# Urgent routings with keys in PSUM and counts against constants, single warming products, a token table written as rows

## The chip, the core and the metric

The kernel runs on one core of a Trainium2 chip. The metric is the device time of one execution in microseconds (us). Engines: PE (TensorE, with its weight loads as PEld), DVE (VectorE), ACT (ScalarE), POOL (GpSimd), SP (SyncE, which starts most DMAs). Each works through its own instructions in the order in which they are written; semaphores hold an instruction back until what it needs is there.

## The reference

Attention over 4 x 8 heads of 576 positions of width 64, mixed with a linear memory by a gate per head, gives 2304 tokens of width 512. A first expert layer routes each token to one of 8 experts, by the largest scores first and with at most 288 tokens an expert; then a gated MLP works on all tokens.

```python
a /= a.sum(-1, keepdims=True) + 1e-09
local = np.matmul(a, v)
g = 1.0 / (1.0 + np.exp(-beta))[None, :, None, None]
return (g * mem_out + (1 - g) * local)
...
order = np.argsort(-flat)                 # all token-expert scores, best first
for idx in order:
    tok, e = (int(idx) // E, int(idx) % E)
    if assigned[tok] >= 0 or counts[e] >= cap:
        continue
    assigned[tok] = e
    counts[e] += 1
...
out[mask] = np.maximum(x[mask] @ w1[e], 0.0) @ w2[e]
...
g = x @ w_gate
return (g / (1.0 + np.exp(-g)) * (x @ w_val)) @ w_out
```

## The kernel before

**Stages.** Attention over 16 pairs of heads runs from 0 to about 249 us. Then the greedy assignment is done in eight phases. Phase `ph` finds, over the scores that are still alive, the expert that fills up next, and its 288 tokens (`route`, L983 on). The tokens of a phase are gathered by an indirect DMA (`xg`), transposed on PE (L1451) to `xt`, and go through that expert's two products. Groups of finished tokens then go through the gated MLP and are scattered to the output. Products of fp32 numbers are made as three products of fp32r parts: `ws` (L1262 on ACT, L1266 on DVE or POOL) holds a weight's upper part and its difference.

**A routing.** The scores become integer keys `kx`, whose upper 16 bits make `h` (L1033), 128 partitions of 160 values. A search in base 4 then finds the key of rank 288, digit by digit: 16 rounds, 8 on the upper half and 8 on the lower. A round counts the keys over three thresholds. One count is a Sign with an accumulator on ACT (L1047), two are comparisons with an accumulator on DVE (L1053). Two products on PE with the stationaries `grp` and `ngrp` add up the counts of an expert's partitions (L1058, L1059). DVE compares the totals with 288 (`kj`, L1063), which adds to the sum found so far (column 3 of `gain`), and makes the next thresholds `th` from it (L1069). After round 7, L1074 turns the keys to the lower half. At the end DVE writes the token numbers, `ix` (L1204), 96 x 3, and SP writes them to the table `tbl` in HBM (L1421), from which the scatters' lists `gi` are read later (L1316).

**Order.** A planner inside the program (`Op`, `Slot`, `schedule`) takes each step with its engine, its duration by a table, what it depends on and which buffer slots it takes, and writes all engines' orders when the program is built. `HARDS` = 2: the first two routings, which nothing can replace, are urgent (`near` in the new code) and their steps go ahead of other work. Buffers in PSUM: `rp` (one tile of 512 columns for all routing steps), `wkp` (three), `acc`. Of the readers and writers of one PSUM tile each waits for the one before it where the program's semaphores order them.

**Warming.** At the start 28 products with `identb` (a unit matrix of bf16, L94) as stationary stand first on PE (L973). In route 1 `warm` (L1271) puts 12 such products as one step, and 2 later, ahead of the first expert's products.

**Start.** DVE makes `ident`, `identb` and other constants, 96 single memsets of `steps` and 16 of `gain` (L111 to L117), the counts' buffers `cn`, and then the gate `gt` from beta (L149 to L156), with one exponential on ACT (L150) between. The first values of `am`, turned by PE in L570, give DVE the scales of the heads (L576 to L579).

Of the kernel before, what the change touches and what calls it, by code (L numbers as in the profile page):

```python
# [9 lines left out]
F32 = mybir.dt.float32  # L10
# [64 lines left out]
def kernel(ctx: ExitStack, tc: tile.TileContext, qt_, kt_, v, M_prev, z_prev, beta,  # L75
# [12 lines left out]
    with tc.tile_pool(name="tmp", bufs=1) as tmp:  # L88
# [4 lines left out]
        identb = cst.tile([128, 128], BF, name="identb")  # L93
        V.tensor_scalar(identb, jp, 0.0, None, op0=OP.is_equal)  # L94
# [12 lines left out]
    steps = [cst.tile([128, 16, 3], F32, name=f"steps{y}") for y in range(2)]  # L107
# [4 lines left out]
    for r in range(16):  # L112
        w = 4.0 ** (7 - r)
        V.memset(gain[:, r, 0:3], w)
        for j in range(3):
            for y in range(2):
                V.memset(steps[y][:, r, j:j + 1], (j + 1) * w - (0.0 if j > y else 0.5 if r < 8 else 2.0 ** -17))  # L117
# [4 lines left out]
    cnts = [[cst.tile([128, 4], BF, name=f"cn{x}{y}") for x in range(2)] for y in range(2)]  # L122
    sgns = [cst.tile([128, 2], BF, name=f"sg{x}") for x in range(2)]
    for y in range(2):
        for x in cnts[y]:
            V.memset(x, float(CAP))
            V.memset(x[:, 0:y + 1], 80.0)
# [331 lines left out]
    with ExitStack() as actx:  # L459
# [5 lines left out]
        G.iota(jw, pattern=[[1, 128]], base=0, channel_multiplier=-1, allow_small_or_imprecise_dtypes=True)  # L465
        maskb = wk.tile([128, 128], BF, name="maskb", bufs=1)
# [521 lines left out]
    def route(ph, prev):  # L988
# [10 lines left out]
        def rp():  # L999
            return Slot("rp", 1)  # L1000
# [26 lines left out]
        def f(e):  # L1027
# [7 lines left out]
        step("A", 0.24, f)  # L1035
# [4 lines left out]
        na = 1  # L1040
        for rd in range(16):
            sp_ = rp()

            def f(e, rd=rd):
                with nc.allow_low_precision(reason="whole numbers up to 160"):
                    for j in range(na):
                        A.activation(t.jk2, t.R, AF.Sign, scale=-1.0, bias=t.th[:, j:j + 1] if rd % 8 else steps[na - 1][:, rd, j:j + 1],  # L1047
                                     accum_out=sgns[rd % 2][:, j:j + 1])
            sgn = Op(None, {"A": 0.49 * na}, f, deps=[last[0]], hard=ph < HARDS, lat=SAFE if ph else 0.0, slack=RND if ph else 0.0)

            def f(e, rd=rd):
                for j in range(na, 3):
                    V.tensor_scalar(t.junk, t.R, t.th[:, j:j + 1] if rd % 8 else (j + 1) * 4.0 ** (7 - rd), None,  # L1053
                                    op0=OP.is_ge, op1=OP.add, accum_out=cnts[na - 1][rd % 2][:, j:j + 1])
            cnt = step("V", (0.37 if rd % 8 else 0.3) * (3 - na), f, lat=SAFE if ph else 0.0, slack=RND if ph else 0.0)

            def f(e, rd=rd):
                PE.matmul(ptile()[:, 0:4], grp, cnts[na - 1][rd % 2], start=True, stop=False)  # L1058
                PE.matmul(t.p[:, 0:na], ngrp, sgns[rd % 2][:, 0:na], start=False, stop=True)  # L1059
            step("PE", 0.08, f, deps=[sgn], take=[sp_])  # L1060
# [5 lines left out]
            if (rd + 1) % 8:  # L1066
                def f(e, rd=rd):
                    t.th = rt.tile([128, 4], F32, name="th", bufs=2)
                    V.tensor_scalar(t.th[:, 0:3], steps[na - 1][:, rd + 1], gain[:, rd + 1, 3:4], None, op0=OP.add, op1=OP.add,  # L1069
                                    accum_out=t.th[:, 3:4])  # L1070
                step("V", 0.22, f)
            elif rd == 7:
                def f(e):
                    V.scalar_tensor_tensor(t.h[2], t.h[1], t.kd[:, 1:2], t.h[0], op0=OP.subtract, op1=OP.add)  # L1074
                    t.R = t.h[2]
                step("V", 0.25, f, deps=[low_], port="V")
# [538 lines left out]
```

## Time and profile before

| | |
|---|---|
| median of three runs | 1049.97 us (1046.54 to 1054.10) |
| the profiled execution | 1046.89 us, of which the span is 1045.1 us |
| busy in the span | PE 925.2 us, DVE 773.2, ACT 591.9, POOL 357.9 |
| TensorE's granted clock | .939 of full speed on average |
| stages | attention to about 249 us, route 0 to 291, route 1 to 346, then experts and groups |

The span is the time from the first to the last instruction that the profile shows. Busy shares are means over stages with different limits: PE's 89% is nearly full after 360 us and low between 250 and 291, so each part of the change is to be held against its own stage.

### The profile page before, as it was taken

How to read it: one execution, taken by the hardware profiler on the slowest of the kernel's cores; microseconds unless marked ns; L12 is line 12 of the kernel's file. 1: busy time of each engine (PE TensorE's matmuls, PEld its weight loads, DVE VectorE, ACT ScalarE, POOL GpSimd, SP SyncE). 2: the span in 40 equal slices, each digit the busy share in tenths (PEclk: the TensorE clock that was granted, in tenths of full speed). 3: DMA queues.
4: the chain of work that ended last, by engine and by line, in shares of the span. 5: the costliest groups of instructions: out<-in, count | busy, mean ns of one | idle time of the engine just before them, and what ended most of it. 6: DMA issues, size and time to landing. Idle time of an engine off the chain costs nothing.

```text
span 1045.1 us, 19428 instructions
## 1 busy us (share of the span) xinstructions
PE 925.2 (89%) x6909; PEld 783.5 (75%) x6909; DVE 773.2 (74%) x2633; ACT 591.9 (57%) x1304; POOL 357.9 (34%) x498
## 2 busy tenths in 40 slices
PE   7689889875168699997999999999999999999995
PEld 4468778774048597775898777899777899888895
DVE  8878888895857788989977676878786766444462
ACT  7758979763445377446566445466544555433552
POOL 4467677750245474455421232230011140000200
PEclk9979999997569699998999999999999999999998
DMA  9569789764462733265350033260032170000100
GB/s 278 109 140 228 166 202 181 167 138 127 140 144 62 184 102 101 61 175 170 120 146 2 1 121 24 95 151 21 1 121 24 44 202 21 1 1 1 41 1 21
DMA packets 130545, 105.37 MB, mean 101 GB/s; under 512 B 99136, under 2 KB 112592, under 8 KB 128400
## 3 DMA queue, kind: packets, MB, share of 16 engines
q1 hardware_dynamic: 120560, 61.14, 24.4%
q0 software_dynamic: 9888, 43.00, 15.4%
q8 instruction: 54, 0.88, 0.4%
q14 instruction: 43, 0.35, 0.1%
HBM read 72.39 MB, written 9.45 MB: 78 GB/s over the span
## 4 chain that ended last, share of the span: by engine, by line
PE 48%; issue 1%; POOL 1%; DMA 1%; DVE 0%; ACT 0%; POOLq 0%
PE wkp L1233 29%; PE acc L1233 18%; DMA xg<-xs,ix 1%; PE wkp L1451 1%; POOL out_dram L1386 1%; PE rp L1197 0%; DVE ws L1266 0%; POOL r L1251 0%; POOL xg L1251 0%; PE rp L1059 0%; PE rp L1058 0%; DVE hd L1484 0%; PE rp L1090 0%; ACT ws L1262 0%; ACT f64r L1381 0%
## 5 line engine op out<-in xcount | busy, mean ns | idle before, releaser
L1233 PE MATMUL wkp<-ya,ws 128*128 128x512 f32 (+1 forms) x864 | 182.4, 364 | 1.3 <-ACT ws L1262 1.3
L1233 PE MATMUL acc<-ws,us 128*128 128x512 f32 x648 | 162.2, 395 | 0.0
L1233 PEld LDWEIGHTS wkp<-ya,ws 128*128 128x128 f32 x864 | 143.4, 192 | 24.3 <-ACT ws L1262 1.4
L1266 DVE TENSOR_TENSOR ws<-m2r,ws 128x512 fp32r<-128x512 f32 x141 | 99.6, 707 | 71.6 <-ACT ws L1262 69.7
L1262 ACT ACTIVATE ws<-m2r 128x512 fp32r<-128x512 f32 x170 | 106.6, 628 | 78.6 <-PE wkp L1233 41.9
L1233 PE MATMUL wkp<-yb,ws 128*128 128x512 f32 x576 | 137.9, 393 | 0.0
L1233 PEld LDWEIGHTS acc<-ws,us 128*128 128x128 f32 x648 | 118.4, 188 | 22.5
L1233 PEld LDWEIGHTS wkp<-yb,ws 128*128 128x128 f32 x576 | 106.4, 188 | 21.1
L1233 PE MATMUL acc<-hd,ws 128*128 128x288 f32 x768 | 120.4, 304 | 0.6 <-DVE hd L1484 0.6
L1233 PE MATMUL wkp<-xt,ws 128*128 128x288 f32 x768 | 120.2, 304 | 0.3 <-DVE xt L1456 0.3
L783 POOL TENSOR_TENSOR pb<-P,pb 128x576 f16<-128x576 f32 (+2 forms) x61 | 93.2, 1529 | 52.4 <-ACT pb L776 43.9
L1233 PEld LDWEIGHTS acc<-hd,ws 128*128 128x128 f32 x768 | 108.9, 193 | 1.8 <-DVE hd L1484 1.2
L1233 PEld LDWEIGHTS wkp<-xt,ws 128*128 128x128 f32 x768 | 109.1, 193 | 1.3 <-DVE xt L1456 0.6
L1262 ACT ACTIVATE ws<-r 128x512 fp32r<-128x512 f32 x128 | 79.6, 645 | 38.2 <-PE acc L1233 12.2
L1266 DVE TENSOR_TENSOR ws<-r,ws 128x512 fp32r<-128x512 f32 x114 | 78.3, 700 | 19.7 <-ACT ws L1262 14.6
L1053 DVE TENSOR_SCALAR_CACHE_REDUCE junk<-h,th 128x160 bf16<-128x160 f32 x224 | 84.8, 379 | 7.0
L1047 ACT ACTIVATE jk<-h,th 128x160 bf16<-128x160 f32 x112 | 47.6, 425 | 59.0 <-DVE th L1069 58.6
L1386 POOL DMA_INDIRECT out_dram<-f64r,gi x18 | 20.0, 1113 | 165.7 <-DVE f64r L1379 119.2
L1343 ACT ACTIVATE sil<-wkp 128x512 f32<-128x512 f32 (+1 forms) x60 | 33.2, 553 | 75.4 <-PE wkp L1233 56.5
L1251 POOL DMA_INDIRECT r<-in_moe_w_dram,wi x32 | 33.5, 1047 | 119.7 <-DVE key L1080 54.8
L452 POOL TENSOR_TENSOR m2r<-f64a,f64r 128x512 int32<-128x512 int32 x34 | 46.6, 1372 | 72.2 <-DVE kj L1063 32.4
L675 PE MATMUL sp<-kt,qt 64*128 64x288 f32 (+4 forms) x576 | 57.0, 324 | 14.4 <-ACT P L720 7.4
(230 smaller groups left out, 1685.3 us busy)
## 6 DMA issues: line engine op xcount, KB each, us to landing
f<-in_moe_w_out_dram SPq DMA_DIRECT2D x12, 512.0 KB, 3.6
f<-in_moe_w_gate_dram SPq DMA_DIRECT2D x11, 512.0 KB, 4.0
f<-in_moe_w_val_dram SPq DMA_DIRECT2D x11, 512.0 KB, 3.5
vr<-in_vb_dram SPq DMA_DIRECT2D x16, 320.0 KB, 4.4
xq<-in_qt_dram SPq DMA_DIRECT2D x16, 288.0 KB, 4.3
xk<-in_kt_dram SPq DMA_DIRECT2D x16, 288.0 KB, 4.0
xs<-X SPq DMA_DIRECT2D x3, 1024.0 KB, 5.1
pt<-pb SPq DMA_TRANSPOSE x49, 4.2
```

Source lines behind the costliest of these rows:

```text
L452: return op({"G": 1.225}, lambda e: G.tensor_tensor(dst.bitcast(I32), t.a, t.r, op=OP.add), [o1] + o4, use=[ra, aa])
L675: PE.matmul(dst, st, mv, start=k not in keys[:j], stop=k not in keys[j + 1:])
L783: lambda e, i=i, c=c: (V if e == "V" else G).tensor_tensor(p.pb[i][:, 1, c], p.P[i][:, c], p.pb[i][:, 0, c], op=OP.subtract), deps=[ho], u ...
L1047: A.activation(t.jk2, t.R, AF.Sign, scale=-1.0, bias=t.th[:, j:j + 1] if rd % 8 else steps[na - 1][:, rd, j:j + 1], accum_out=sgns[rd % 2] ...
L1053: V.tensor_scalar(t.junk, t.R, t.th[:, j:j + 1] if rd % 8 else (j + 1) * 4.0 ** (7 - rd), None, op0=OP.is_ge, op1=OP.add, accum_out=cnts[n ...
L1233: PE.matmul(dst, st(x), mv(y), start=first and t == 0, stop=last and t == 2)
L1251: G.indirect_dma_start(out=dst, out_offset=None, in_=src, in_offset=bass.IndirectOffsetOnAxis(ap=idx, axis=0))
L1262: A.activation(h.t[:, 0], raw(), AF.Copy)
L1266: (V if e == "V" else G).tensor_tensor(h.t[:, 1], raw(), _f(h.t[:, 0]), op=OP.subtract)
L1343: A.activation(t.sl, t.g[0][:, 0:n], AF.Silu)
L1386: put = G.indirect_dma_start(out=out, out_offset=bass.IndirectOffsetOnAxis(ap=self.gi[:, q:q + 1], axis=0), in_=t.o, in_offset=None)
L1451: PE.transpose(t.p[:, TW * j:TW * j + TW], x.xg[:, j, c:DM:4], ident[0:TW, 0:TW])
```

## The change

In the two urgent routings the thresholds `th` are no longer made in 14 of the 16 rounds. DVE counts where the key less the sum so far is at least a constant of `steps`, by a SCALAR_TENSOR_TENSOR whose second tensor is one column read 160 times. ACT's Sign takes the sum as its bias and reads `xs`, a copy of the negated keys with the round's constant added, which ACT makes anew in each round (L1071 of the new program, an added instruction). The keys `t.R` lie in columns 0 to 160, later 256 to 416, of one PSUM tile, and the round's products go to columns 480 or 496 of the same tile. `steps` exists once, not twice, with 48 memsets; of the buffers `cn` two remain. `identb` is built in the attention part, after `jw`. `warm` makes each product a step of its own, with `grp` as stationary. `ix` is made a second time as floats (`ixf`), turned on PE to 3 x 96, copied to integers (`rows`), and written to the table in three rows of 96 numbers.

```diff
-        identb = cst.tile([128, 128], BF, name="identb")
-        V.tensor_scalar(identb, jp, 0.0, None, op0=OP.is_equal)
...
-    steps = [cst.tile([128, 16, 3], F32, name=f"steps{y}") for y in range(2)]
+    steps = cst.tile([128, 16, 3], F32, name="steps")
...
+        identb = wk.tile([128, 128], BF, name="identb", bufs=1)
+        V.tensor_scalar(identb, jw, 0.0, None, op0=OP.is_equal)
...
+            if near:
+                ptile()
+                t.pk, t.hs, t.h[1] = t.p, list(t.h), t.p[:, 0:160]
...
+                    if past:
+                        A.activation(t.jk2, t.xs, AF.Sign, bias=gain[:, rd, 3:4], accum_out=sgns[rd % 2])
+                    else:
+                        A.activation(t.jk2, t.R, AF.Sign, scale=-1.0, bias=t.th[:, 0:1] if rd % 8 else steps[:, rd, 0:1],
+                                     accum_out=sgns[rd % 2])
...
+                    if past:
+                        V.scalar_tensor_tensor(t.junk, t.R, gain[:, rd, 3:4], steps[:, rd, j:j + 1].to_broadcast([128, 160]),
+                                               op0=OP.subtract, op1=OP.is_ge, accum_out=cnts[rd % 2][:, j:j + 1])
...
+            if near and (rd + 1) % 8:
+                def f(e, rd=rd):
+                    t.xs = t.hs[1 + rd % 2]
+                    A.activation(t.xs, t.R, AF.Copy, scale=-1.0, bias=4.0 ** (6 - rd) - (0.5 if rd < 8 else 2.0 ** -17))
+                base = Op(None, {"A": 0.24}, f, deps=[sgn], hard=True, use=[sk])
...
+                t.p = t.pk[:, 480 + 16 * (rd % 2):] if near else ptile()
+                PE.matmul(t.p[:, 0:4], grp, cnts[rd % 2], start=True, stop=False)
+                PE.matmul(t.p[:, 0:1], ngrp, sgns[rd % 2], start=False, stop=True)
...
-            if (rd + 1) % 8:
+            if (rd + 1) % 8 and not near:
...
+                    if near:
+                        t.h[2] = t.pk[:, 256:416]
...
+            V.tensor_scalar(r.ixf, t.p3[0:TW, 0:3], float(N // 2), None, op0=OP.add)
...
-            for _ in range(n):
-                PE.matmul(p, identb, onesb[:, None, :].to_broadcast([128, 4, 128]), start=True, stop=True)
-        pe(0.24 * n, f, deps, take=[w0])
+        for x in range(n):
+            def f(e, x=x):
+                if x == 0:
+                    t.p = work().rearrange("p (a b) -> p a b", a=4)
+                PE.matmul(t.p, grp, onesb[:, None, :].to_broadcast([128, 4, 128]), start=True, stop=True)
+            o = pe(0.24, f, deps, take=[] if x else [w0], use=[w0] if x else [])
+            deps = [o]
...
+                PE.transpose(t.p[0:3, 0:TW], self.r.ixf, ident[0:TW, 0:TW])
...
+                V.tensor_copy(t.r, t.p[0:3, 0:TW])
...
+                tbl[CAP * s:CAP * s + CAP].rearrange("(a b) -> a b", b=TW), t.r), deps=[o], use=[rs])
```

**Where instructions move.** DVE at the program's start, before (line, operation, written tile <- read tiles, shape):

```order
L92 TENSOR_SCALAR ident<-jp 128x128
L94 TENSOR_SCALAR identb<-jp 128x128
L96 TENSOR_SCALAR before<-jp 128x128
L98 MEMSET onesb 128x128
L101 TENSOR_SCALAR jmod<-jmod 128x128
L103 TENSOR_SCALAR grp<-jmod 128x128
```

The new DVE order holds, of these, all but `identb` at the start; here it follows the last steps of the gate:

```order
L150 TENSOR_SCALAR gt<-gt 128x8
L151 TENSOR_SCALAR gt<-gt 128x8
L152 RECIPROCAL gt<-gt 128x8
L159 MEMSET alive 128x18
L161 MEMSET vw 128x16
L463 TENSOR_SCALAR identb<-jw 128x128
L465 TENSOR_SCALAR maskb<-jw 128x128
```

`identb` has moved from the second of DVE's rows behind six rows of the gate `gt`, which wait for ACT's exponential.

DVE in the first rounds of route 0, before (in brackets the engines whose semaphores a row waits for):

```order
L1053 TENSOR_SCALAR junk,cn_204<-h_4760 128x160 [waits Activation_49]
L1053 TENSOR_SCALAR junk,cn_204<-h_4760 128x160 [waits DVE_49]
L1063 SCALAR_TENSOR_TENSOR kj,gain<-rp,gain 128x4 [waits PE_49]
L1069 TENSOR_SCALAR th<-steps_84,gain 128x3 [waits DVE_49]
L1053 TENSOR_SCALAR junk,cn_205<-h_4760,th 128x160 [waits DVE_49] x2
```

ACT there in the new program; `rp` is the PSUM tile of the keys, `sg` the sums of the Signs, `f64a` and `f64r` conversions of other weights:

```order
L1035 ACTIVATE rp<-kx 128x160 [waits DVE_49,Activation_49]
L1052 ACTIVATE jk_4709,sg_155<-rp,steps 128x160 [waits Activation_49]
L1071 ACTIVATE h_4705<-rp 128x160 [waits DVE_49]
L1039 ACTIVATE h_4704<-kx 128x160
L1050 ACTIVATE jk_4709,sg_156<-h_4705,gain 128x160 [waits DVE_49]
L1071 ACTIVATE h_4706<-rp 128x160 [waits DVE_49,PE_49]
L440 ACTIVATE f64a<-f_4690 128x512 [waits DMAHW2_49]
L434 ACTIVATE f64r<-f_4690 128x512
```

On PE there, in the new program, the round's products wait for ACT alone:

```order
L1009 MATMUL rp<-ident,vw 128x128 [waits DVE_49,PE_49]
L1076 LDWEIGHTS grp
L1076 MATMUL rp<-cn_153,grp 128x4 [waits Activation_49]
L1077 LDWEIGHTS ngrp
L1077 MATMUL rp<-sg_155,ngrp 128x1
```

The row `th` is gone from DVE, and ACT has gained a row of L1071 in each round, which waits for DVE's counts and which PE's pair waits for.

PE in route 1, before, at the first round's pair:

```order
L1011 MATMUL rp<-ident,vw 128x128
L1058 LDWEIGHTS grp
L1058 MATMUL rp<-cn_204,grp 128x4
L1059 LDWEIGHTS ngrp
L1059 MATMUL rp<-sg_208,ngrp 128x1
L1278 LDWEIGHTS identb
L1278 MATMUL wkp<-onesb,identb 128x512
```

The twelve products of L1278 follow one another there, and the next pair stands behind the twelfth. In the new program:

```order
L1300 LDWEIGHTS grp
L1300 MATMUL wkp<-onesb,grp 128x512
L1076 LDWEIGHTS grp
L1076 MATMUL rp<-cn_153,grp 128x4
L1077 LDWEIGHTS ngrp
L1077 MATMUL rp<-sg_155,ngrp 128x1
L1300 LDWEIGHTS grp
L1300 MATMUL wkp<-onesb,grp 128x512
```

Four products now stand ahead of the first pair, four between it and the second, and four behind that; three of the nine transposes of gathered tokens then stand ahead of the third pair, where nine did.

## Rows read from the trace of the kernel before

**Rows 1.** Windows of the span: us, busy us of each engine (instructions), PE's granted clock, DMA.

```profile
250.00:291.00 41.00, 6.05 (x54) 4.30 (x54) 35.37 (x197) 18.84 (x52) 8.12 (x11) 0.52 0.41 128
360.00:440.00 80.00, 79.67 (x443) 67.85 (x442) 69.66 (x236) 55.16 (x122) 43.73 (x59) 0.97 0.35 109
440.00:490.00 50.00, 41.51 (x201) 31.62 (x201) 42.23 (x173) 28.50 (x71) 24.48 (x32) 0.90 0.59 170
```

**Rows 2.** Timeline of the start: us, duration, engine, line, operation, [idle before it <-releaser].

```profile
1.82 8.08 PE L973 MATMUL T<-onesb,identb 128*128 128x512 bf16 x28 [1.82 <-DVE onesb L98]
9.94 0.29 PE L570 MATMUL T<-ident,am 128*128 128x128 f32 x1
5.62 3.79 PEld L973 LDWEIGHTS <-identb 128*128 128x128 bf16 x18 [0.28 <-issue]
6.33 0.21 ACT L150 ACTIVATE gt<-gt 128x8 f32<-128x8 f32 x1 [0.89 <-DVE gt L149]
7.42 0.20 DVE L156 RECIPROCAL gt<-gt 128x8 f32<-128x8 f32 x1
11.78 0.28 DVE L576 TENSOR_REDUCE am<-T 128x1 f32<-128x128 f32 x1
```

**Rows 3.** Waits from 10 to 249 us: total us, times, longest; the row on a DMA.

```profile
PEld L844 <- DMA pt<-pb: 3.9, 3, 2.6
```

**Rows 4.** Timeline of one round of route 0, and `kj` of its last round.

```profile
253.67 0.16 DVE L1063 SCALAR_TENSOR_TENSOR kj<-rp,gain 128x4 f32<-128x4 f32 x1 [0.32 <-PE rp L1059]
254.13 0.38 DVE L1053 TENSOR_SCALAR_CACHE_REDUCE junk<-h,th 128x160 bf16<-128x160 f32 x1
254.19 0.43 ACT L1047 ACTIVATE jk<-h,th 128x160 bf16<-128x160 f32 x1 [0.79 <-DVE th L1069]
254.56 0.38 DVE L1053 TENSOR_SCALAR_CACHE_REDUCE junk<-h,th 128x160 bf16<-128x160 f32 x1
255.01 0.19 PE L1058 MATMUL rp<-cn,grp 128*128 128x4 bf16 x1 [1.39 <-DVE junk L1053]
255.27 0.16 DVE L1063 SCALAR_TENSOR_TENSOR kj<-rp,gain 128x4 f32<-128x4 f32 x1 [0.32 <-PE rp L1059]
255.48 0.21 DVE L1069 TENSOR_SCALAR_CACHE_REDUCE th<-steps,gain 128x3 f32<-128x3 f32 x1
255.73 0.38 DVE L1053 TENSOR_SCALAR_CACHE_REDUCE junk<-h,th 128x160 bf16<-128x160 f32 x1
280.11 0.15 DVE L1063 SCALAR_TENSOR_TENSOR kj<-rp,gain 128x4 f32<-128x4 f32 x1
```

**Rows 5.** One line's instructions (durations in ns: least, median, most), then groups by line and shape.

```profile
L1074 DVE SCALAR_TENSOR_TENSOR h<-h,kd,h x8: 380/385/1265, 266.0 to 797.1; 128x160 f32<-128x160 f32 x8
...
L1024 DVE TENSOR_TENSOR kx<-vb,kx 128x160 int32<-128x160 int32 x8 | 2.6, 326 | 0.3
...
L1539 DVE TENSOR_TENSOR yb<-acc,yb 128x160 fp32r<-128x160 f32 x4 | 1.2, 318 | 0.0
...
L1536 ACT ACTIVATE yb<-acc 128x160 fp32r<-128x160 f32 x4 | 1.2, 305 | 0.0
```

**Rows 6.** Timeline of route 1: warming block, `kj` behind it, gathered tokens, last round.

```profile
294.06 5.27 PE L1278 MATMUL wkp<-onesb,identb 128*128 128x512 bf16 x12
299.44 0.16 DVE L1063 SCALAR_TENSOR_TENSOR kj<-rp,gain 128x4 f32<-128x4 f32 x1 [3.91 <-PE rp L1059]
304.59 0.41 ACT L1454 ACTIVATE xt<-wkp 128x288 fp32r<-128x288 f32 x1 [9.29 <-PE wkp L1451]
305.31 0.21 PE L1058 MATMUL rp<-cn,grp 128*128 128x4 bf16 x1
336.40 0.16 DVE L1063 SCALAR_TENSOR_TENSOR kj<-rp,gain 128x4 f32<-128x4 f32 x1 [0.50 <-PE rp L1059]
```

**Rows 7.** Transposes of the gathered tokens (ns: least, median, most); `ws` differences on DVE.

```profile
L1451 PE MATMUL wkp<-ident,xg x96: 246/286/437, 301.5 to 857.8; 96*128 96x96 f32 x96
...
L1266 DVE TENSOR_TENSOR ws<-m2r,ws 128x512 fp32r<-128x512 f32 x141 | 99.6, 707 | 71.6 <-ACT ws L1262 69.7
```

More of the change, by code (lines that the diff above doesn't have):

```diff
@@ L1041, in route @@
         for rd in range(16):
-            sp_ = rp()
-            def f(e, rd=rd):
[L1045 to L1059, printed above, removed]
@@ L1060, in route, with f @@
-            step("PE", 0.08, f, deps=[sgn], take=[sp_])
+            sp_ = sk if near else rp()
+            past = near and rd % 8 > 0
+            def f(e, rd=rd, past=past):
+                with nc.allow_low_precision(reason="whole numbers up to 160"):
+                    if past:
[3 more added lines that the diff above has]
+                                     accum_out=sgns[rd % 2])
@@ new lines, in route, with f @@
+            sgn = Op(None, {"A": 0.49}, f, deps=[last[0], base], hard=near, lat=SAFE if ph else 0.0, slack=RND if ph else 0.0,
+                     use=[sk] if near and not past else [])
+            def f(e, rd=rd, past=past):
+                for j in (1, 2):
+                    if past:
+                        V.scalar_tensor_tensor(t.junk, t.R, gain[:, rd, 3:4], steps[:, rd, j:j + 1].to_broadcast([128, 160]),
+                                               op0=OP.subtract, op1=OP.is_ge, accum_out=cnts[rd % 2][:, j:j + 1])
+                    else:
+                        V.tensor_scalar(t.junk, t.R, t.th[:, j:j + 1] if rd % 8 else (j + 1) * 4.0 ** (7 - rd), None,
+                                        op0=OP.is_ge, op1=OP.add, accum_out=cnts[rd % 2][:, j:j + 1])
@@ L1062, in f @@
+            step("PE", 0.08, f, deps=[sgn], take=[] if near else [sp_], use=[sk] if near else [])
             def f(e, rd=rd):
@@ L1073, in f @@
                 def f(e):
+                    if near:
+                        t.h[2] = t.pk[:, 256:416]
                     V.scalar_tensor_tensor(t.h[2], t.h[1], t.kd[:, 1:2], t.h[0], op0=OP.subtract, op1=OP.add)
                     t.R = t.h[2]
-                step("V", 0.25, f, deps=[low_], port="V")
+                step("V", 0.35 if near else 0.25, f, deps=[low_], port="" if near else "V", use=[sk] if near else [])
         def f(e):
@@ L1203, in f @@
             r.ix = rt.tile([TW, 3], I32, name="ix", bufs=8)
+            r.ixf = rt.tile([TW, 3], F32, name="ixf", bufs=2)
             V.tensor_scalar(r.ix, t.p3[0:TW, 0:3], float(N // 2), None, op0=OP.add)
-        r.idx = step("V", 0.07, f, use=[s3], slack=RSL)
+            V.tensor_scalar(r.ixf, t.p3[0:TW, 0:3], float(N // 2), None, op0=OP.add)
+        r.idx = step("V", 0.14, f, use=[s3], slack=RSL)
         return r
@@ L1420, in __init__, with f @@
             self.g1.append(gath(4.3, lambda e: load1(e, 1), [self.r.wix], after=late_, take=[r1[1]]))
-            self.told = Op(None, {"D": 0.5}, lambda e: SP.dma_start(
-                tbl[CAP * s:CAP * s + CAP].rearrange("(a b) -> b a", b=TW), self.r.ix), deps=[self.r.idx])
+            ws, rs, t = Slot("wkp", 3), Slot("rows", 1), type("T", (), {})()
+            def f(e):
+                t.p = work()
+                PE.transpose(t.p[0:3, 0:TW], self.r.ixf, ident[0:TW, 0:TW])
+            o = Op(None, {"PE": 0.12}, f, deps=[self.r.idx], after=late_ and [self.g1[1].g], take=[ws])
+            def f(e):
+                t.r = rt.tile([3, TW], I32, name="rows")
+                V.tensor_copy(t.r, t.p[0:3, 0:TW])
+            o = Op(None, {"V": 0.17}, f, deps=[o], take=[rs], use=[ws])
+            self.told = Op(None, {"D": 0.2}, lambda e: SP.dma_start(
+                tbl[CAP * s:CAP * s + CAP].rearrange("(a b) -> a b", b=TW), t.r), deps=[o], use=[rs])
             self.w2 = []
```

26 lines of the change are left out of this document (12 added, 14 removed).

## Prediction

> **What bounds the kernel now.** I read the table of windows first, stage by stage. Up to about 249 us all engines run through one attention schedule, each in a written order. From 360 us on PE is nearly always busy: 79.67 of 80.00 us in 360 to 440, though only 41.51 of 50.00 in 440 to 490 [rows 1]. Between them PE is mostly idle: 6.05 us of work in 41.00 during the first urgent routing [rows 1]. There the chain of a routing round sets the time, not any engine's load. So three things can move the end: when attention gets going, how long the chains of the two urgent routings take, and what PE itself has to do after 360. A shift of the first two arrives whole at the expert work, since its tokens wait for the routings; off PE, a change after 360 costs only where PE waits for it.
>
> **Start: `identb` comes late.** Before, PE's 28 warming products begin at 1.82 and the transpose of L570 follows at 9.94 [rows 2]. In the new order DVE makes their stationary `identb` only behind the sigmoid chain of `gt`, so all 28 wait for that chain. It can't be early: ACT was ready for the exponential .89 us ahead of 6.33 [rows 2], at 5.44. DVE, with 48 memsets fewer, will be there by then. So the last step of the chain, at 7.42 before [rows 2], moves to 6.53, and `identb`, three rows further on, is there at about 6.9; PE begins at about 7.0, 5.2 us later than at 1.82. If its products take what they took, L570's transpose comes at 15.1. DVE read its result at 11.78 [rows 2], after other work; now it waits until about 15.7. That is **+4.0 us**: behind that row stand, on DVE, the scales of the first heads, on ACT `vh`, which is made with them, and so the whole first pair. Bounds: PE's products run at two speeds, the last 18 at .21 us each (3.79 for 18 weight loads [rows 2], the 2.4 GHz level), the first at about twice that; were all 28 at .21, they would end 2.2 us earlier, so +1.8 at least; +5.2 if DVE's other work slips too. Does the slip survive to 249? Only a schedule that waits for loads would take it up. Between 10 and 249 us the largest wait of PE's side for a DMA is 3.9 us, for `pt<-pb` [rows 3], which is attention's own product and slips with it. So I let it pass whole.
>
> **A round of the urgent routings.** Before, undisturbed, counts begin at 254.13 and at 255.73: 1.60 us. It is .43 to the second count, .45 to the pair of products, .26 to `kj` at 255.27, .21 to `th`, .25 to the next count [rows 4]. The edit drops `th`, **−.25**: the count follows `kj` at the .21 at which `th` did. The new count is a SCALAR_TENSOR_TENSOR over 160 columns; one such stands in the trace with a median of 385 ns [rows 5], where the old one has .38 [rows 4]: at most +.02 for two.
>
> Reading keys from PSUM: a DVE TENSOR_TENSOR with one PSUM source and 160 columns takes 318 ns, one with SBUF alone 326 [rows 5]. I charge nothing. The difference, .008, is small; four times it on all 64 counts would be 2.0 us, which I keep as a bound.
>
> The Trainium skill (Perfetto Trace Analysis, "Optimizing Scalar/DVE Operations") puts the overhead of a DVE access at about 60 ns on SBUF and 125 on PSUM. By it 64 counts would cost 64 × .065 = 4.2 us more, an estimate from that page; the two rows here show no such surcharge, and the measurement decides.
>
> What the diff doesn't say is the wait that the bank brings. The keys lie in the same PSUM tile as the round's products, and the order with its waits shows PE's pair waiting for ACT's new Copy, which waits for DVE's second count. So the Copy stands in the chain. Its price: an ACTIVATE from PSUM with 160 columns takes 305 ns [rows 5], and I add .04 for one hand-over more. A round is now .21 + .44 + .455 + .345 + .26 = 1.71: **+.11 where −.23 was to be had**. 14 such rounds a route: +1.5. In rounds 0 and 8 the Sign reads the PSUM keys too and DVE's counts wait for it: .43 [rows 4], with its hand-over about .55, and the Copy's .345 on top: +.9 each, +1.8. Part of this returns. Route 0's `kj` run from 253.67 to 280.11, 15 rounds in 26.44 [rows 4], 1.76 each and not 1.60, since DVE's conversions stand between them; these 2.4 us can now lie under Copy and products. I take 1.3 back: **route 0 +2.0 us**, bounds 0 (all hidden, rounds 0 and 8 at half their price) and +3.5 (nothing hidden).
>
> **Route 1.** Before, PE has twelve warming products in one block from 294.06, for 5.27 us, and round 1's pair sits behind it: `kj` at 299.44 waited 3.91 us for PE [rows 6]. Round 2's Sign stood behind ACT's `xt` at 304.59, which had waited 9.29 us for PE's transposes of gathered tokens, and its pair came at 305.31 [rows 6]. Now the products come in fours, with pairs between them, and the Sign stands ahead of `xt`. But round 2's pair still follows three transposes of the gathered tokens, so most of the 3.91 is lost to the same gather, and the pair comes at about 304.4, 1 us earlier. From there to the last `kj` at 336.40 [rows 6] a round takes 2.4 us, as PE's product blocks and ACT's queue stand in the way. Following the new order with these durations the later pairs stand behind smaller blocks, and the last comes 2 to 4 us earlier, though ACT has .31 more in each round. I take **−3.0**, bounds −6 (the freed 3.91 and the 1 us kept, and another from the later rounds) and +3 (ACT late by .2 in each of 14 rounds).
>
> **After 360.** There are eight transposes of 3x96 for the table. The nearest row, 96x96, has a median of 286 ns [rows 7], with loads overlapped by others; I take .19, for 7 where PE is full: **+1.3**, bounds 0 and 2. Eight `ixf` and eight copies to `rows` on DVE lie under PE. The table written as rows lies under the expert work, since no engine waits for it before the last scatters: 0. Last, the planner moved work: DVE makes 33 more of the `ws` differences (141 become 166 on one path and 114 become 122 on the other, by the order), POOL fewer. At .71 each [rows 7] that is 23 us more for DVE. DVE has 10.3 us free of 80 in 360 to 440 and 7.8 of 50 in 440 to 490 [rows 1], and about ten of the 33 fall there. PE already loses 8.5 us in the second window, so it could lose a few more or fewer: 0, bounds −4 and +8.
>
> **Sum.** 4.0 + 2.0 − 3.0 + 1.3 = +4.3. The profiled execution has 1046.9, so 1051.2. The median of the three runs, 1050.0, lies 3.1 above that execution; I put the forecast between the two bases, at **1053 us**.
>
> **Rivals.**
> *The edits do what they say* (faster). The Copy ends before PE needs the counts, a round loses .23, 3.2 us a route, and route 1 gains its 6 in all; with the start slip at 1.8 that is 1.8 − 3.2 − 6 + 1.3 = −6.1: 1041, and 1036 with 3 to 4 us of PE's stalls in 440 to 490 gone. Against it: the waits in the order. It holds if a round is under 1.55 us.
> *The start slip is taken up inside attention.* 4.3 − 4.0: 1047 to 1050. For it: every engine idles somewhere in attention. Against: hardly a row there waits for an input.
> *DVE becomes the bound after 360* (slower). The ten added differences in 360 to 490 delay PE's operands by .71 each, 7 us, and as much again where conversions queued behind them feed POOL late: 4.3 + 7 to 14: 1058 to 1067. It decides from 14 us of idle PE in the window that answers to 440 to 490. For it: DVE is 84% busy there. Against: POOL is relieved of the same work.
> *PSUM reads are dear for DVE.* .03 a count, as bounded above: +2.0, 1055.
>
> **How the numbers follow.** Forecast .45, edits as they say .13, slip taken up .20, DVE bound .17, dear PSUM .05. A measurement of this kernel can tell about 1%, 10.5 us, from no change. Faster by over 1% is under 1039.5: the lower part of the first rival and the favourable ends of the forecast's bounds, .10. Slower by over 1% is over 1060.5: most of the DVE rival and the forecast's upper tail, .17. Within: .73. The range 1041 to 1063 leaves out the deep part of the first rival and the top of the DVE rival, about .2; the forecast's own range is 1047 to 1059.
>
> **What would show it.** The first product on PE at about 7.0 and DVE's `am` near 15.7; attention's last row 4 us later; ACT's Copy between counts and products in each urgent round, and rounds of 1.7 us where nothing interferes; the last `kj` of route 0 some 6 us later than before, that of route 1 some 3. Wrong would be rounds under 1.55, an unchanged end of attention, or over 14 us of idle PE in the window that answers to 440 to 490.

## The result

The changed kernel is faster, by 1.0%. Twenty runs of each gave medians of 1038.41 us against 1049.05 us before; the ratio is .9902, with a 95% interval from .9879 to .9924. I had forecast 1053 us, practically no change, with 1041 as the lower end. The profiled execution of the changed kernel has a span of 1037.6 us, that of the kernel before 1045.1.

The profile after, windows: us, busy us of PE, PEld, DVE, ACT and POOL with instructions, PE's granted clock, DMA share, GB/s.

```profile
253.00:295.00 42.00, 5.82 (x54) 4.42 (x54) 32.86 (x167) 22.43 (x66) 7.73 (x11) 0.50 0.38 120
360.00:440.00 80.00, 76.03 (x426) 63.41 (x426) 75.21 (x264) 54.65 (x125) 23.16 (x32) 1.00 0.30 93
440.00:490.00 50.00, 47.60 (x240) 37.22 (x240) 44.02 (x176) 31.10 (x72) 21.59 (x29) 0.97 0.52 170
```

Against [rows 1]: the first urgent routing looks as before (5.82 us of PE's work, against 6.05; this window begins 3 us later). PE has lost 3.6 us of work between 360 and 440 and gained 6.1 between 440 and 490, and DVE is fuller in both. PE's granted clock in these two windows went from .97 to 1.00 and from .90 to .97 of full speed.

The start, in the timeline of the changed kernel:

```profile
7.24 8.05 PE L971 MATMUL T<-onesb,identb 128*128 128x512 bf16 x28 [7.24 <-DVE identb L463]
15.12 0.27 PE L568 MATMUL T<-ident,am 128*128 128x128 f32 x1
...
15.43 0.29 DVE L574 TENSOR_REDUCE am<-T 128x1 f32<-128x128 f32 x1 [2.67 <-PE T L568]
```

The three times came out as forecast, to .3 us: first product at 7.24 (7.0), the transpose at 15.12 (15.1), `am` at 15.43 (15.7) after 2.67 us of waiting. Against 11.78 in [rows 2] that is +3.65.

One round of route 0 in the changed kernel, and the last `kj`:

```profile
259.09 0.16 DVE L1081 SCALAR_TENSOR_TENSOR kj<-rp,gain 128x4 f32<-128x4 f32 x1 [0.75 <-PE rp L1077]
...
259.30 0.38 DVE L1060 SCALAR_TENSOR_TENSOR junk<-rp,gain,steps 128x160 bf16<-128x160 f32 x1
...
259.73 0.38 DVE L1060 SCALAR_TENSOR_TENSOR junk<-rp,gain,steps 128x160 bf16<-128x160 f32 x1
...
260.21 0.30 ACT L1071 ACTIVATE h<-rp 128x160 f32<-128x160 f32 x1
...
260.57 0.16 PE L1076 MATMUL rp<-cn,grp 128*128 128x4 bf16 x1 [1.59 <-ACT h L1071]
...
260.88 0.16 DVE L1081 SCALAR_TENSOR_TENSOR kj<-rp,gain 128x4 f32<-128x4 f32 x1 [0.42 <-PE rp L1077]
...
284.15 0.15 DVE L1081 SCALAR_TENSOR_TENSOR kj<-rp,gain 128x4 f32<-128x4 f32 x1
```

The Copy of L1071 (260.21) stands between the second count (259.73) and the products (260.57). A round takes 1.79 us here, where it took 1.60 undisturbed in [rows 4], and 12 of the 15 steps from `kj` to `kj` take 1.78 or 1.79; the other three are the last round of each half, which has no Copy (1.32 and 1.62), and round 8 (2.47). The route's 15 steps take 26.84 us, 26.44 before. The conversions (L442 here) lie under the wait.

Now the row that I had not looked at: the gathers of tokens, `xg`. Each answer has the gather's issue on POOL and its time from issue to landing. Before:

```profile
L1251 POOL DMA_INDIRECT xg<-xs,ix x24: 908/927/1453, 291.5 to 843.5; - x24
...
DMA to landing us min/median/max: 7.0/9.3/10.8
```

After:

```profile
L1273 POOL DMA_INDIRECT xg<-xs,ix x24: 906/925/1448, 295.6 to 835.5; - x24
...
DMA to landing us min/median/max: 3.0/3.4/8.6
```

The median gather lands 3.4 us after its issue, not 9.3. The same view for the table, before and then after:

```profile
L1421 SPq DMA_DIRECT2D tbl<-ix x8: 305/321/338, 291.3 to 839.4; - x8
...
DMA to landing us min/median/max: 6.0/8.1/10.9
```

```profile
L1456 SPq DMA_DIRECT2D tbl<-rows x8: 232/247/323, 303.6 to 879.9; - x8
...
DMA to landing us min/median/max: 2.1/2.6/3.1
```

The first write of the table, issued at 291.3 before, went out just ahead of the first gather, at 291.5; now it is issued at 303.6, when that gather has landed.

To see where the 7.5 us between the two profiled executions went, I cut each at the same five instructions: the first product of the first routing, `ix` of routes 0 and 1, the first product of the first group (`wkp<-ya`), and the last of that group's 288 products of this kind, all of which stand in each trace. The times of these rows give each stage's length in us:

| kernel | attention | route 0 | route 1 | to the group | its 288 products | rest of the span | span |
|---|---|---|---|---|---|---|---|
| before | 250.9 | 40.2 | 54.8 | 42.8 | 113.0 | 543.4 | 1045.1 |
| changed | 253.4 | 41.7 | 49.0 | 44.7 | 105.4 | 543.4 | 1037.6 |
| forecast, difference | +4.0 | +2.0 | −3.0 | part of +1.3 | 0 | part of +1.3 | +4.3 |
| measured, difference | +2.6 | +1.5 | −5.8 | +1.9 | −7.6 | 0 | −7.5 |

The start and route 0 stand about where they were put. Route 1 and the group's products make the result. The group's start moves within the order, so the two stages behind route 1 are best read together: 155.9 us before, 150.1 after.

### The profile page after: what moved, and what is told of

Same layout as the page of the kernel before. It is cut to its first block, busy times and chain, and to the rows that moved or that the text cites. A ratio compares the mean times of both kernels' runs of the same rounds, so it can differ in the third digit from the quotient of the medians.

```text
span 1037.6 us, 19343 instructions
## 1 busy us (share of the span) xinstructions
PE 923.2 (89%) x6917; PEld 785.0 (76%) x6917; DVE 783.5 (76%) x2575; ACT 598.6 (58%) x1331; POOL 312.2 (30%) x432
## 4 chain that ended last, share of the span: by engine, by line
PE 71%; DVE 17%; ACT 7%; issue 2%; DMA 1%; POOL 1%; ACTq 0%; SPq 0%; DVEq 0%; POOLq 0%
PE wkp L1255 37%; PE acc L1255 21%; PE sp L673 3%; PE O L842 2%; DVE ws L1288 2%; ACT P L723 2%; DVE nm L709 2%; DVE junk L1060 1%; PE T L971 1%; PE wkp L1486 1%; DVE f64a L445 1%; DVE nm L707 1%; PE T L902 1%; PE T L807 1%; ACT P L718 1%
## 5 line engine op out<-in xcount | busy, mean ns | idle before, releaser
L1255 PE MATMUL wkp<-ya,ws 128*128 128x512 f32 (+1 forms) x864 | 179.7, 361 | 2.7 <-DVE xt L1491 2.2
L1288 DVE TENSOR_TENSOR ws<-m2r,ws 128x512 fp32r<-128x512 f32 x166 | 115.6, 696 | 69.8 <-ACT ws L1284 67.5
L1284 ACT ACTIVATE ws<-m2r 128x512 fp32r<-128x512 f32 x170 | 106.6, 628 | 80.3 <-PE wkp L1255 41.6
L1284 ACT ACTIVATE ws<-r 128x512 fp32r<-128x512 f32 x128 | 80.0, 647 | 40.8 <-PE acc L1255 15.1
L1288 DVE TENSOR_TENSOR ws<-r,ws 128x512 fp32r<-128x512 f32 x122 | 87.5, 730 | 15.8 <-ACT ws L1284 14.0
L448 POOL TENSOR_TENSOR m2r<-f64a,f64r 128x512 int32<-128x512 int32 x34 | 45.5, 1339 | 113.6 <-DVE f64a L445 45.7
L1366 ACT ACTIVATE sil<-wkp 128x512 f32<-128x512 f32 (+1 forms) x60 | 33.2, 553 | 74.8 <-PE wkp L1255 54.9
L1409 POOL DMA_INDIRECT out_dram<-f64r,gi x18 | 22.6, 1254 | 172.0 <-DVE f64r L1402 119.4
L1063 DVE TENSOR_SCALAR_CACHE_REDUCE junk<-h,th 128x160 bf16<-128x160 f32 x168 | 63.5, 378 | 4.9
L673 PEld LDWEIGHTS sp<-kt,qt 64*128 64x128 f32 x576 | 47.0, 198 | 24.6 <-ACT P L718 11.3
```

Of the source, the lines that this page charges most:

```text
L448: return op({"G": 1.225}, lambda e: G.tensor_tensor(dst.bitcast(I32), t.a, t.r, op=OP.add), [o1] + o4, use=[ra, aa])
L673: PE.matmul(dst, st, mv, start=k not in keys[:j], stop=k not in keys[j + 1:])
L1255: PE.matmul(dst, st(x), mv(y), start=first and t == 0, stop=last and t == 2)
L1284: A.activation(h.t[:, 0], raw(), AF.Copy)
L1288: (V if e == "V" else G).tensor_tensor(h.t[:, 1], raw(), _f(h.t[:, 0]), op=OP.subtract)
L1366: A.activation(t.sl, t.g[0][:, 0:n], AF.Silu)
```

## The experiments

Each was timed beside the kernel before on the same chip, in five rounds; ratios are to the kernel before. Three theories stood against one another. *Table*: the old write of the table, ahead of the gathers, holds them back, and everything else is nearly free or costs. *Warming*: route 1 gains because its pairs no longer stand behind a block. *Routing*: the dropped step pays.

### Each part alone

**The table alone.** The kernel before with the table's write of the changed one. Room in SBUF was needed for it: `steps` once, and `identb` late, with `grp` as stationary of the first products and of the warming block.

```diff
...
-                tbl[CAP * s:CAP * s + CAP].rearrange("(a b) -> b a", b=TW), self.r.ix), deps=[self.r.idx])
...
+                tbl[CAP * s:CAP * s + CAP].rearrange("(a b) -> a b", b=TW), t.r), deps=[o], use=[rs])
...
```

> The kernel before with the table alone written as rows (to make room, steps once, and identb late with grp as stationary of the first products, which leaves the start as it was). If the write of single words is what holds the gathers back, xg lands 3 to 4 us after its issue instead of 9 to 10, no transpose waits for xg, the second route takes some 3 us less from ix to ix, and the order, in which DVE makes 30 more ws differences as in the changed kernel, loses its stalls around 440 to 490: 1037 to 1042. If the gain is the warming's or the routing's: 1047 to 1051, with the landing of xg changed or not.

Measured: 1037.85 us, ratio .9863 (.9817 to .9909). Gathers land 3.2 us after their issue (median), route 1 takes 50.2 us, the stage up to the group 40.8 and its products 110.8. This part alone gives about what the whole change gives; the two intervals overlap.

**All but the table.** The changed kernel with the old write.

```diff
...
-                tbl[CAP * s:CAP * s + CAP].rearrange("(a b) -> a b", b=TW), t.r), deps=[o], use=[rs])
...
+                tbl[CAP * s:CAP * s + CAP].rearrange("(a b) -> b a", b=TW), self.r.ix), deps=[self.r.idx])
...
```

> The changed kernel with the old table write. If the single words hold the gathers back: xg lands 9 to 10 us after its issue, the second route loses 3 us or more of its gain, stalls come back after 434, and the time is 1048 to 1055. If warming or routing carry the gain: 1037 to 1041.

Measured: 1067.67 us, ratio 1.0153 (1.0107 to 1.02). Gathers land after 10.0 us again, route 1 takes 54.9 us, the group's products 122.7 and the rest of the span 549.6. Without the table's part the change is a loss, and a larger one than expected.

**The routing alone**: the kernel before with the new counts, the Copy and the keys in PSUM, and the constants that go with them.

> The kernel before with the new counts in the two urgent routings alone. By the chain of waits a round of route 0 takes 1.78 us as in the changed kernel, route 0 is 1 to 2 us longer than before, and the time is 1048 to 1053. If the dropped step is what pays: 1040 to 1044.

Measured: 1063.38 us, ratio 1.0112 (1.006 to 1.0164). Route 0 takes 41.7 us, 1.5 more than before, as the chain of waits says. The time lies above both expectations: most of the loss stands behind the routes, 8.5 us in the stage up to the group and 7.4 in the rest, where the planner's order has changed and the gathers land late (median 9.9 us). What makes this order dear with late gathers stays open.

**The warming alone**: the kernel before with single products.

```diff
...
-            for _ in range(n):
-                PE.matmul(p, identb, onesb[:, None, :].to_broadcast([128, 4, 128]), start=True, stop=True)
-        pe(0.24 * n, f, deps, take=[w0])
...
+            o = pe(0.24, f, deps, take=[] if x else [w0], use=[w0] if x else [])
...
```

> The kernel before with single warming products alone. If the second route gained because its pairs no longer stand behind a block, it takes 3 to 6 us less from ix to ix and the time is 1043 to 1047. If the gather sets it, round 2 still waits for xg until about 304 us and the time is 1048 to 1051.

Measured: 1058.28 us, ratio 1.0061 (1.0028 to 1.0093). That is above both expectations. Route 1 takes 55.7 us, no less than before, and PE waits for the gather longer; the profiled execution loses the rest behind it, 5.7 us in the group's products and 7.2 in the rest of the span. The first row is of the kernel before, the second of this one, in the waits of PE from 245 to 360 us.

```profile
PE wkp L1451 <- DMA xg<-xs,ix: 8.1, 5, 2.4
```

```profile
PE wkp L1452 <- DMA xg<-xs,ix: 13.8, 5, 5.5
```

So with a late gather the freed time goes to the gather, as the prediction had it. What it lacked was that the gather itself would come early.

### Packets, place or order

The table's part changes three things at once: the packets of the write, its place (behind the gather, since PE and DVE must turn the numbers first), and the planner's order, in which DVE gets 30 more of the `ws` differences. The next four kernels separate them. The first three have PE, DVE, ACT and POOL in exactly the order of the kernel they start from, and SP too except for the write's own form.

**Before, 12 bytes a packet.** Same order as before; the three numbers of a partition go side by side, so 96 packets replace 288. The table's numbering is permuted by it, and with it the places of the output's rows; the sizes of all other transfers stay.

```diff
-                tbl[CAP * s:CAP * s + CAP].rearrange("(a b) -> b a", b=TW), self.r.ix), deps=[self.r.idx])
+                tbl[CAP * s:CAP * s + CAP].rearrange("(b a) -> b a", b=TW), self.r.ix), deps=[self.r.idx])
```

> The kernel before in the same order on every engine; only the table is written with the three numbers of a partition side by side, 96 packets of 12 bytes for 288 of 4 (so the table's numbering, and with it the place of the output's rows, is permuted). If packets ahead of the gather hold it back: xg lands 5 to 7 us after its issue, the second route takes 2 to 4 us less from ix to ix, and the time is 1040 to 1046. If the order made the gain: xg lands as before or the time stays at 1048 to 1053.

Measured: 1035.83 us, ratio .9848 (.9798 to .9898), faster than either expectation. The order of the engines is untouched, so the order isn't what makes the gain. Route 1 takes 49.2 us, 5.6 less; the stage up to the group 39.8, 3.0 less.

**Before, spaced.** Same order, the same 288 packets of 4 bytes at the same place, but a number every 8 bytes in HBM.

```diff
-    tbl = drm.tile([N], I32, name="tbl")
+    tbl = drm.tile([N, 2], I32, name="tbl")
...
+                tbl[CAP * s:CAP * s + CAP, 0].rearrange("(a b) -> b a", b=TW), self.r.ix), deps=[self.r.idx])
```

> The kernel before in the same order; only the table in HBM is spaced out, a number every 8 bytes, so the same 288 packets from 96 partitions go out ahead of the gather. If their number ahead of the gather holds it back: xg lands 9 to 10 us after its issue, its first transpose comes 10 us after ix, and the time is 1048 to 1056. If it is that neighbouring words of 4 bytes from different partitions meet at one place in HBM: xg lands in 3 to 7 us and the time is 1036 to 1044.

Measured: 1035.14 us, ratio .984 (.9805 to .9875). So the number of packets isn't what costs the time either: the same 288 do no such harm when they don't lie side by side in HBM. What the DMA queues moved in the 10 us that follow the first `ix` shows it (queue, kind: packets, MB, share of 16 engines; q0 carries the gathers of tokens and of weights). The kernel before, from 291.09; then spaced, from 288.46; then 12 bytes, from 288.39:

```profile
q0 software_dynamic: 114, 0.38, 74.2%
q1 hardware_dynamic: 448, 0.53, 17.8%
```

```profile
q0 software_dynamic: 268, 0.90, 67.7%
q1 hardware_dynamic: 448, 0.53, 18.9%
```

```profile
q0 software_dynamic: 406, 1.69, 68.1%
q1 hardware_dynamic: 256, 0.53, 19.9%
```

With the old write the gathers' queue gets 114 packets through while it is busy for 74% of the time, by this view; with the same number of words spaced out it gets 268 through in 68%, with 12-byte packets 406. So spacing frees the queue less than larger packets do, and route 1 takes 51.8 us with it against 49.2; the whole time doesn't tell the two apart. In the spaced kernel PE's wait for `xg` between 245 and 360 us falls from 8.1 us, shown above, to

```profile
PE wkp L1451 <- DMA xg<-xs,ix: 1.9, 3, 1.1
```

Which property of the old write does it is not settled. That a packet's neighbours in HBM come from other partitions isn't enough, since this holds for the 12-byte packets too. How many packets fall into a stretch of HBM puts the three in the order that the queue shows: in 24 bytes they are 6, 3 and 2. No run separates this from direct neighbourhood of single words.

**After, words.** The changed kernel's order and place, with the table spaced out so that each number is a packet of its own.

```diff
...
-                tbl[CAP * s:CAP * s + CAP].rearrange("(a b) -> a b", b=TW), t.r), deps=[o], use=[rs])
+                tbl[CAP * s:CAP * s + CAP, 0].rearrange("(a b) -> a b", b=TW), t.r), deps=[o], use=[rs])
```

> The changed kernel in the same order on every engine; only the table in HBM is spaced out, so that each token number goes as a packet of its own, 288 a write, as before the change. If the single words themselves hold the other transfers back: gathers or weight loads near a write land 3 to 6 us later and the time is 1043 to 1055. If the position of the write (now behind the gather) or the order of the engines made the gain: within 3 us of the changed kernel, 1036 to 1041.

Measured: 1038.08 us, ratio .9855 (.9819 to .9892): no loss. It has 288 packets a write too, but decides neither number nor place: spaced words do no harm at the early place, and at the late one even the old kind does little, as the next run shows.

**After, the old kind at the late place.** DVE copies the numbers at the late place and the old pattern writes them.

```diff
-                t.r = rt.tile([3, TW], I32, name="rows")
-                V.tensor_copy(t.r, t.p[0:3, 0:TW])
+                t.r = rt.tile([TW, 3], I32, name="rows")
+                V.tensor_copy(t.r, self.r.ix)
...
-                tbl[CAP * s:CAP * s + CAP].rearrange("(a b) -> a b", b=TW), t.r), deps=[o], use=[rs])
+                tbl[CAP * s:CAP * s + CAP].rearrange("(a b) -> b a", b=TW), t.r), deps=[o], use=[rs])
```

> The changed kernel with the write at its late place (DVE copies the numbers there), but written as before the change: 288 words from 96 partitions, neighbours in HBM from different partitions. If the place of the write, behind the gather, is what counts: 1036 to 1042, and xg lands as in the changed kernel. If the kind of the write counts wherever it stands: the weight gathers issued around it land late and the time is 1043 to 1056.

Measured: 1041.06 us, ratio .9877 (.9847 to .9906). The old write behind the gather costs little or nothing: the intervals of this and of the changed kernel overlap. Its own landing takes 6.7 us (median) against 2.6, but nobody waits for it. Either cure is enough, a write that isn't made of single words side by side, or one that goes out behind the gather; the change has both.

### The terms that came out right, tested

**An early start.** The changed kernel with `grp` as stationary of the first products.

```diff
-            PE.matmul(T.rearrange("p (a b) -> p a b", a=4), identb, onesb[:, None, :].to_broadcast([128, 4, 128]), start=True, stop=True)
+            PE.matmul(T.rearrange("p (a b) -> p a b", a=4), grp, onesb[:, None, :].to_broadcast([128, 4, 128]), start=True, stop=True)
```

> The changed kernel with grp as stationary of the first 28 products, so that PE doesn't wait for the late identb. If the late start cost what the trace shows at the end of attention (2.5 to 3 us): PE's first product at about 2 us, attention ends 2 to 3 us earlier, time 1034 to 1037. If the start is taken up later: 1037 to 1041.

Measured: 1037.08 us, ratio .984 (.9803 to .9878). PE starts at 2.03 instead of 7.24, but attention in the profiled execution ends at 256.8, later than in the changed kernel (253.4). This execution doesn't settle the term: its granted clock from 0 to 250 us was .91 of full speed, where the changed kernel's was .94. All profiles together say more. Eight kernels with an early stationary, five with `identb` as before and three with `grp`, end attention at 247.4, 248.1, 248.1, 249.8, 250.9, 251.0, 251.5 and 256.8 (this one); six with the late `identb` at 251.7, 251.8, 252.4, 253.4, 253.5 and 260.6. The two far values have the two lowest granted clocks, .91 and .90; the other twelve have .93 to .95, and among them every late start ends later than every early one. Their middle values, 249.8 and 252.4, differ by 2.6 us, less than the 4 forecast. Two executions with the same order and nearly the same granted clock still differ by 2.8 us (250.9 and 248.1).

**Keys in SBUF.** The changed kernel with the keys in SBUF, so that neither the products nor the counts wait for the Copy.

```diff
-                ptile()
-                t.pk, t.hs, t.h[1] = t.p, list(t.h), t.p[:, 0:160]
+                t.xs = t.h[2]
...
-                t.p = t.pk[:, 480 + 16 * (rd % 2):] if near else ptile()
+                ptile()
```

> The changed kernel with the keys in SBUF and the round's products in a PSUM tile of their own, in the same order: the products no longer wait for the Copy. If the bank's waits hold the round: a round of route 0 falls from 1.78 to 1.4 us where nothing interferes, rounds 0 and 8 lose .9 each, the last kj of route 0 comes 4 to 7 us earlier, and the time is 1031 to 1035. If ACT's own work (Sign and Copy) holds it: a round stays over 1.65 and the time is 1037 to 1041.

Measured: 1038.04 us, ratio .9828 (.9782 to .9874), and route 0 takes 41.2 us, only .5 less. Both expectations were too simple. A round with nothing beside it does take 1.35 us, as these two rows show (1.57 to 1.62 where ACT's conversions hold back its Sign):

```profile
254.60 0.16 DVE L1076 SCALAR_TENSOR_TENSOR kj<-rp,gain 128x4 f32<-128x4 f32 x1 [0.32 <-PE rp L1072]
...
255.95 0.16 DVE L1076 SCALAR_TENSOR_TENSOR kj<-rp,gain 128x4 f32<-128x4 f32 x1 [0.32 <-PE rp L1072]
```

But some rounds take far longer. At 261.38 a count takes 1.25 us while POOL adds from 261.14 on:

```profile
261.14 1.31 POOL L448 TENSOR_TENSOR m2r<-f64a,f64r 128x512 int32<-128x512 int32 x1 [20.80 <-DVE kj L1076]
...
261.38 1.25 DVE L1057 SCALAR_TENSOR_TENSOR junk<-h,gain,steps 128x160 bf16<-128x160 f32 x1
```

The counts by line (ns: least, median, most), with the keys in SBUF, with the keys in PSUM, and those of the kernel before:

```profile
L1057 DVE SCALAR_TENSOR_TENSOR junk<-h,gain,steps x56: 373/385/3294, 254.8 to 333.3; 128x160 bf16<-128x160 f32 x56
```

```profile
L1060 DVE SCALAR_TENSOR_TENSOR junk<-rp,gain,steps x56: 362/384/385, 257.5 to 333.6; 128x160 bf16<-128x160 f32 x56
```

```profile
L1053 DVE TENSOR_SCALAR_CACHE_REDUCE junk<-h,th x224: 364/379/382, 254.1 to 822.5; 128x160 bf16<-128x160 f32 x112
```

The same operation, the same 56 instructions: up to 3294 ns with the keys in SBUF, never over 385 with the keys in PSUM. Eleven of the 56 with keys in SBUF took over 450 ns, and each of them ran beside a TENSOR_TENSOR of POOL; with keys in PSUM 19 of the 56 ran beside such a TENSOR_TENSOR and none was longer. The old count, which reads one 160-column tensor from SBUF and no second one, never took over 382 ns either, with 77 of its 256 beside one: the new form of the count brought the danger, and PSUM took it away. So the bank's wait costs .44 us in each quiet round, 1.79 against 1.35, and PSUM keeps the counts clear of POOL's work; in the two routes' length the two nearly cancel (41.2 and 51.2 us with SBUF, 41.7 and 49.0 with PSUM).

**Without the new routing.** The kernel of the table alone with single warming products as well, beside the changed kernel itself on one chip.

> The kernel before with the table as rows and single warming products (with grp in the first products too), but with its old counts and thresholds: the changed kernel without its new routing. If the new routing costs, as it did alone with the old table (a ratio of 1.011): this is .5 to 1% faster than the changed kernel on the same chip, 1028 to 1034 where the changed kernel has 1038. If the loss came only with the late gather: the two are within .5%.

> The changed kernel itself, beside the one without its new routing on the same chip: 1036 to 1042 if it stands to the kernel before as it did (.990); where the routing costs, it is .5 to 1% slower than the other.

Measured: 1038.43 us, ratio .9864 (.9823 to .9905), and 1041.23 us, ratio .989 (.9846 to .9935). They differ by .3%, within what the runs can tell. Route 0 is .9 us longer with the new routing (41.6 against 40.7), route 1 is 3.0 shorter (47.1 against 50.2), the stage up to the group 5.4 longer and its products 8.0 shorter. With a gather that lands early, the new routing is neither a gain nor a loss that can be seen.

The kernels from .983 to .986 can't be told from each other. The smallest edit among them, the spaced table in the old kernel, has .984; against the changed kernel's first comparison (.9902, from .9879) its interval, up to .9875, stands clear, against the second (.989, from .9846) it doesn't.

## Why the prediction was wrong

**The table, put at 0: here the prediction failed.** The step read: "The table written as rows lies under the expert work, since no engine waits for it before the last scatters: 0." It asked who waits for the write and not whom the write holds up. It was also the one DMA whose neighbours on the queues I didn't read. The trace of before had it: the table goes out at 291.28 on SP, the gather at 291.53 on POOL, and gathers take 9.3 us to land, for which PE's transposes wait 8.1 us. The runs put this term at −1.4 to −1.6% by itself (.9863, .9848, .984), 14 to 17 us, by a write that no longer holds the gathers back. The rival "the edits do what they say" came near the time by luck: its condition, rounds under 1.55 us, didn't hold.

**Route 1, −3.0: wrong by the same step.** I took the gather as fixed ("most of the 3.91 is lost to the same gather"). Its first transpose came 10.4 us after `ix` before (301.53 against 291.09) and 7.25 after the change (302.37 against 295.12), so round 2's `kj` stood 8.1 us behind `ix` and not 14.6. That gives −5.8 in all, just inside the bound of −6, for which the freed time had to be kept. The table alone gives −4.6 of it (50.2 us). With the old table and single products the route took 55.7 us: there the reasoning about the late gather holds.

**After 360, 0 with bounds −4 and +8: +1.9 up to the group and −7.6 in its products, −5.7 together.** This too is mainly the table's. The two stages take 155.9 us before, 150.3 and 151.0 in the two kernels with before's order and a harmless table, and 149.5 to 152.0 in all eight others whose gathers aren't held back; with the old write ahead of the gathers and another order they take 162.8 to 167.4. What the order does is to move time between the two: with the new routing the group starts later (44.6 to 45.7 us after `ix`, against 39.8 to 40.8) and its products end sooner (103.7 to 105.6 us, against 110.5 to 111.7). So PE's waits for DVE's counts in the window from 440 to 490, 7.1 us before, are gone in the changed kernel; the first row is of before, the second all that is left after, in the waits of PE there:

```profile
PE rp L1058 <- DVE junk L1053: 7.1, 4, 3.0
```

```profile
PE wkp L1255 <- DVE xt L1491: 2.2, 1, 2.2
```

The kernel with 12-byte packets, in before's order, keeps 6.4 us of such waits (425 to 500 us) and has nearly the same sum. The eight new transposes take 246 ns each (median) and show in no stage. The rival in which 33 more differences make DVE the bound fell (its sum, 4.3 + 7 to 14, gives 1058 to 1065 from the execution's 1046.9, not 1067): DVE has 44.02 us of work in 440 to 490, where it had 42.23, and PE idles 2.4 us there, where it idled 8.5.

**Without the table.** The forecast's other terms don't sum to what the other edits cost: the kernel with the old table lost 1.5%, about 16 us, against +4.3, and its profile has 17.8 us of the loss behind the two routes. Of the signs named as wrong, rounds under 1.55, an unchanged end of attention and over 14 us of idle PE, none appeared, so they couldn't have shown this error. The last `kj` of route 0 came 4.0 us later, not 6, and that of route 1 2.1 us earlier, not 3 later.

**The start, +4.0: right in place, less in size.** The rows of the start agree to .3 us; at the end of attention 2.6 us were left, in these two profiles as in the middle values of twelve. "So I let it pass whole" is not borne out; where the missing 1.4 us went is not shown, and single executions differ by more.

**Route 0, +2.0: right.** Measured +1.5 in the changed kernel and in the routing alone. The round was put at 1.71 and takes 1.79 through; .08 was missing in the hand-overs. The conversions hid fully, more than the 1.3 us that I gave back. Rounds 0 and 8 were put at +.9 each. From the routing's first product to the first `kj` it is 3.87 us and was 2.79, +1.08; round 8 takes 2.47 and took 1.91, +.56. (By its own terms, 14 × .11 and 1.8, the upper bound is 3.3, not 3.5.)

**PSUM reads, no charge: right.** The count's median is 384 ns from PSUM and 385 from SBUF. The Trainium skill (Perfetto Trace Analysis, "Optimizing Scalar/DVE Operations") gives a DVE access about 60 ns of overhead on SBUF and about 125 ns on PSUM; that difference doesn't show in this operation's duration. A rule that I had not weighed does bear on the other rows. The Trainium skill (SBUF — State Buffer, "Who interferes with whom") says that a DVE instruction with two inputs in SBUF contends with a GpSimd instruction that reads SBUF, and one with a single such input, outside the two-port modes, does not. The traces agree: the counts with two inputs there took up to 3294 ns, those with their keys in PSUM never over 385. The prediction's own row for the operation had a sign of it: its longest, 1265 ns [rows 5], ran beside a TENSOR_TENSOR of POOL.

## What to carry to other kernels

A DMA that nobody waits for is not free: ask which transfer is issued behind it, and how long that one takes to land. The row to read is the time from issue to landing of the awaited transfer and the packets that its queue gets through meanwhile, before any argument about engines. Where an order can shift work from one stage to the next, read the two stages together. When a change has several parts, the one with the smallest text in the plan may carry the whole result; here the other parts cost about 1.5% as long as that one was missing.

## What the runs showed of the hardware

288 packets of 4 bytes, written side by side in HBM from 96 partitions, held the gathers behind them to 114 packets in 10 us, where the same 288 packets spaced at 8 bytes let 268 through and 96 packets of 12 bytes 406. A gather's landing fell from 9.3 to 3.4 us (medians) when the write changed kind and place. What on the path to HBM makes words side by side slow, and whether it is the neighbourhood or the number of packets in a stretch, is not shown by these runs. The Trainium skill (DMA: Bandwidth & Descriptors, "Specifications") has transfers under 512 bytes done as read-modify-write. All writes of the table here are under that, with packets of 4 or 12 bytes, and of 384 in the changed kernel's rows, so this rule alone doesn't tell the slow one from the quick ones.

A SCALAR_TENSOR_TENSOR of 160 columns with its operands in SBUF took between 373 and 3294 ns, the long ones beside POOL's work; with its main operand in PSUM it stayed between 362 and 385 ns in all 56 instances, 19 of them beside a TENSOR_TENSOR of POOL.
